# Fused attention and two expert layers on one core: one-hot work spread over more groups, the maxima's row written in two halves, gate steps moved forward

## The chip, the core and the metric

The kernel runs on one core of one Trainium2 chip. The metric is the device time of one launch in microseconds (us). The core has five engines with queues of their own: TensorE (PE, with its weight loads as PEld), VectorE (DVE), ScalarE (ACT), GpSimd (POOL) and SyncE (SP, which here only issues DMAs). Each engine takes its instructions in the order in which the program issues them, and waits on semaphores for the others.

## The reference

The kernel computes three layers in one launch: an attention whose queries are pooled in twos, a layer that sends each token to its best expert (2,304 tokens, 8 experts), and a soft mixture of experts over the result.

```python
q_pool = q.reshape(B, H, S // 2, 2, D).mean(axis=3)            # B=4, H=8, S=1152, D=64
scores = scale * np.matmul(q_pool, k.transpose(0, 1, 3, 2))
scores = scores - np.max(scores, axis=-1, keepdims=True)
attn = np.exp(scores); attn = attn / (attn.sum(-1, keepdims=True) + 1e-9)
x = (attn @ v) -> [B * S/2, H * D]                             # 2304 tokens of 512
logits = x @ w_gate + modality_bias[modality_id]; e = argmax(logits)
x = gate_w[:, None] * (relu(x @ w1[e]) @ w2[e])                # each token, its expert alone
return soft_moe(x)                                             # dispatch and combine by softmax
```

## The kernel before

**Tiling.** The attention goes over 16 pairs of heads, p = 0 to 15, four pairs to a batch (HP = 4), so pairs 0, 4, 8 and 12 are the first of their batches. A pair has 36 positions, pos = 0 to 35: two halves of the queries (u), nine blocks of 128 keys (c), two heads (j). At each position the program issues two matmuls for the scores (S1 at line 251 and S2 at line 257, both into one `sc` bank), the exponential on ScalarE (line 261), then whatever the table `work` holds for that position, then one step from `queue`, then one-hot steps, and, at positions 2, 8, 14, 20, 26 and 32, a group: twelve P·V matmuls (line 271) and three additions on GpSimd for the row sums (line 284). Everything is issued by hand in this order, and each engine keeps it.

**The maxima.** While pair p is worked on, the row maxima of the scores of later pairs are found in 27 pieces each: a matmul into a bank `mps` (lines 197 to 202) and a reduction by VectorE (line 204). At positions 29, 30, 31, 33, 34 and 35 of pairs 1 to 13 the pieces belong to pair p+2. At position 29 `maxred` puts the maxima of pair p+1 together, and at position 32 `maxrow` turns them with two transposes into a bank `nps` (line 220) and writes them with three multiplications by a mask into five rows of QL, which S2 of pair p+1 reads: one of 1024 columns for both heads (line 222), then one of 64 columns for each head (line 225). In pair 0 this happens at position 35, three positions later, as the `late` of line 566 says.

**The banks.** `mps`, `nps`, and the banks of `fin0` (`sg`), `fin1` (`sgT`), `fin2` (`tp`), `ranks` (`rp`) and `table` (`tbp`) are tiles with the one tag `mx`, of which there are three. They are handed out in turn: the fourth tile asked for takes the bank of the first and its first matmul waits until the first has been read for the last time. At position 33, behind the maxima's piece, `fin2(p, 0)` takes such a bank, in pairs that are not the first of their batch.

**Routing.** Behind the last pair of a batch, at position 18 (RT) of pairs 4, 8 and 12, `route` hands out the small steps that choose the experts of that batch's tokens, and `in_order` puts them into `queue`: `choose` (logits, their maximum, the winner), `gates` (an exponential on ScalarE, four small steps on VectorE, the last of which writes into `xr`, and a DMA that stores `xr` into `xs`), `place` (`ranks` with nine small matmuls, five small steps on VectorE, 24 one-hot steps on ScalarE at lines 372 and 373, and `table` with six matmuls), and `count` (two small steps on VectorE, lines 409 and 410). `rest` stands for empty steps. From `queue` one step is issued at positions with pos % 3 < 2 in pairs 4, 8, 12 and behind 12, and at even positions from 8 on in the others. One-hot steps are no callables of the queue; they are taken four at a time ahead of a group. The first two batches thus send their 24 one-hot steps into the groups at positions 26 and 32 of pair 5 (9) and 2, 8, 14 and 20 of pair 6 (10), and `table` and `count` come behind them at positions 22, 24 and 26 of pair 6 (10). `fin2(p - 1, 0)` at position 7 (FC) of pairs 5, 9 and 13 writes into the next batch's `xr`, of which there is one buffer.

Of the kernel before, what the change touches and what calls it, by code (L numbers as in the profile page):

```python
# [17 lines left out]
HP = H // 2  # L18
# [19 lines left out]
HPOS = 4  # L38
NI = N // 128
NB = E * (N // TS)  # L40
NHOT = 4
XW = DM + 8
QSTEP = 2
GS = 3
LAG = 3
# [11 lines left out]
MR = (29, 32)  # L57
# [4 lines left out]
RT = 18  # L62
# [23 lines left out]
def attention(ctx, tc, g):  # L86
# [8 lines left out]
    V = nc.vector  # L95
# [16 lines left out]
    mask = cp.tile([69, 5, 128], F32, name="mask")  # L112
    wgbd = cp.tile([128, HP, 2 * E], F32, name="wgbd")
    ahead = g["ahead"] = Ahead(tc, g, KS, KH, QS, QL, KX, QX, KC, KL, QLc, QC, VT)
    pairs = [(b, hp) for b in range(B) for hp in range(HP)]
    n = len(pairs)
# [18 lines left out]
    def load_v(p):  # L135
        b, hp = pairs[p]
        nc.sync.dma_start(out=st[p]["v"], in_=vT[b, hp])
# [77 lines left out]
    def maxrow(p):  # L215

        ql = st[p]["QL"]
        nps = ps.tile([128, 512], F32, name="nps", tag="mx", bufs=3)
        for j in range(2):
            nc.tensor.transpose(nps[:69, j * 128:(j + 1) * 128], MXZ[:, j, :], ident)  # L220
        nv = nps[64:69, 0:256].rearrange("p (j c) -> p j c", j=2)
        V.tensor_mul(ql[64:69, :, 0:512].rearrange("p j (a c) -> p j a c", a=4),  # L222
                     nv.unsqueeze(2).to_broadcast([5, 2, 4, 128]), mask[64:69, 0:4].unsqueeze(1).to_broadcast([5, 2, 4, 128]))
        for j in range(2):
            V.tensor_mul(ql[64:69, j, 512:576], nv[:, j, 64 * j:64 * j + 64], mask[64:69, 4, 0:64])

    def maxrow0(p, spans):

# [57 lines left out]
    def group(p, g_):  # L286
        steps = range(GS * g_, GS * g_ + GS)
        for step in steps:
            PV(p, step)
        for step in steps:  # L290
            if (p, step) != (n - 1, 2 * NKB - 1):
                accadd(p, step)
# [129 lines left out]
    def in_order(r, select=None):  # L422
        choose, place, count, gates = r

        rest = [lambda: None] * 3
        if select is None:
            return choose[:4] + rest[:2] + gates + choose[4:] + rest[:1] + place + count
        expert, rows = select
        place = place[:1] + count + rest + expert + [lambda i=i: ahead.fetch(i) for i in range(2)] + place[1:]
        return choose[:3] + rest + gates + choose[3:] + rest + place + rows[:1] + rest + rows[1:]  # L430

    def first():

# [100 lines left out]
    nc.sync.dma_start(out=wgbd[0:64, :, 0:E], in_=wg[0])  # L534
    nc.sync.dma_start(out=wgbd[64:128, :, E:2 * E], in_=wg[1])
    consts = g["route_consts"]()
    queue = []
    for p in range(n + 1):
        work = {}

        def at(pos, *fs):
            work[pos] = work.get(pos, []) + list(fs)

        mp = lambda q, m: (lambda: maxpiece(q, m))
        NP = len(pieces)
        if p == 0:
            for i, m in enumerate(range(NP0, NP)):
                at(P0[0] + i * P0[1] // 8, mp(0, m))
            at(P0[0] + P0[1] + 1, lambda: maxred(0, [3, 4]))
            at(P0[0] + P0[1] + 2, lambda: maxrow0(0, [(288, 384), (384, 512), (512, 576)]))  # L550
            for i, m in enumerate([24, 25, 26] + list(range(24))):
                at(P1[0] + i * P1[1] // NP, mp(1, m))
            for i in range(3):
                at(33 + i, mp(2, 24 + i))
        elif p + 1 < n:
            for pos, m in zip(MA1, range(24)) if p == 1 else zip(MA, range(3, 24)):
                at(pos, mp(p + 1, m))
            if p + 2 < n:
                for pos, m in zip(MB, (24, 25, 26, 0, 1, 2)):
                    at(pos, mp(p + 2, m))  # L560
        if p + 2 < n:
            for pos, f in zip(PREP0 if p == 0 else PREP, prep(p + 2, nc.gpsimd if p == 0 or p >= HP and p % HP < 2 else None)):
                at(pos, f)
        if p < n:
            if p + 1 < n:
                late = 3 if p == 0 else 0
                at(MR[0] + late, lambda: maxred(p + 1, [0, 1, 2, 3, 4]))
                at(MR[1] + late, lambda: maxrow(p + 1))
            late = 4 if p in (0, n - 1) else 2 if p >= HP and p % HP == 0 else 0
            at(FA[0] + late, lambda: fin0(p, 0))  # L570
            at(FA[1] + late, lambda: fin1(p, 0))
            if pairs[p][1]:
                at(FA[2], lambda: fin2(p, 0))
        if p > 0:
            if pairs[p - 1][1] == 0:
                at(FC, lambda: fin2(p - 1, 0))
            fb = FE if p < 4 else FB if p < n - HP else FZ
            at(fb[0], lambda: fin0(p - 1, 1))
            at(fb[1], lambda: fin1(p - 1, 1))
            if p < n:  # L580
                at(fb[2], lambda: fin2(p - 1, 1))
                if pairs[p - 1][1] == HP - 1:
                    at(RT, lambda: queue.extend(in_order(route(pairs[p - 1][0]), ahead.select() if p == n - HP else None)))
        if p == n - 2:
            for i in range(2, 6):
                at(AF2[i - 2], lambda i=i: ahead.fetch(i))
            for i in range(6):
                at(6 * i + 2, lambda i=i: ahead.split(i))
        if p == n - 1:
            at(0, lambda: ahead.fetch(6), lambda: ahead.fetch(7))  # L590
            at(14, lambda: ahead.load_x(0), lambda: ahead.load_x(1))
            at(26, lambda: ahead.turn(0))
            at(28, lambda: ahead.turn(1))
            at(29, ahead.gates)
            for i in range(6):
                at(6 * i + 2, lambda i=i: ahead.split(6 + i))
        if p == n:
            group(n - 1, 2 * NKB // GS - 1)
            assert not queue
            mm, ev = ahead.mm, ahead.ev  # L600

            def both(*fs):
                return [f[i] for i in range(max(map(len, fs))) for f in fs if i < len(f)]

            mm(0)
            ev(0)
            fin0(n - 1, 1)
            mm(1)
            fin1(n - 1, 1)
            ev(1)  # L610
            choose, place, count, gates = route(B - 1)
            ta, tb = g["make_tasks"](ps, count)
            rest = gates[1:]
            run = lambda fs: [f() for f in fs]
            run(choose[:3])
            mm(2)
            run(both(choose[3:], gates[:1]))
            fin2(n - 1, 1)
            ev(2)
            mm(3)  # L620
            place[0]()
            ta[0]()
            ev(3)
            mm(4)
            mm(5)
            table = place.pop()
            chain = both(place[1:], ta[1:], rest)
            for i, f in enumerate(chain):
                f()
                if i in TAIL:  # L630
                    u = 4 + TAIL.index(i)
                    ev(u)
                    if u < 6:
                        mm(u + 2)
            mm(8)
            mm(9)
            table()
            mm(10)
            tb[0]()
            cut = lambda u: (lambda: ahead.split(u))  # L640
            g["rest"] = [cut(12), cut(13), lambda: mm(11), cut(14), cut(15)] + [lambda u=u: mm(u) for u in range(12, 16)] + [lambda: ev(15)]
            break

        units = [(u, c, j) for u in range(2) for c in range(NKB) for j in range(2)]
        for z in units[:3]:
            S1(p, *z)
        for pos, z in enumerate(units):
            if pos >= 3:
                S1(p, *z)
            S2(p, *z)  # L650
            for f in work.get(pos, []):
                f()
            if p and pos % CST == 0 and consts:
                consts.pop(0)()
            if queue and pos >= (8 if p < n - 3 else 0) and (pos % 3 < 2 if p % HP == 0 or p > n - HP else pos % QSTEP == 0) and callable(queue[0]):
                queue.pop(0)()
            if pos % (2 * GS) == LAG - 1:
                for _ in range(NHOT):
                    if queue and not callable(queue[0]):
                        queue.pop(0)[1]()  # L660
            if pos == LAG - 1 and p > 0:
                group(p - 1, 2 * NKB // GS - 1)
            elif pos >= 2 * GS and pos % (2 * GS) == LAG - 1:
                group(p, pos // (2 * GS) - 1)
            if pos == 3 and p + 3 < n:
                if p == 0:
                    load_v(2)
                load(p + 3)
# [1085 lines left out]
```

## Time and profile before

| | us |
|---|---|
| median of 3 runs (lowest, highest) | 811.82 (810.58, 812.17) |
| profiled execution, its own time | 811.47 |
| span of its trace, first to last instruction | 809.8 |
| TensorE busy | 779.9 (96% of the span) |
| VectorE busy | 566.6 (70%) |
| GpSimd busy | 544.2 (67%) |
| ScalarE busy | 461.5 (57%) |
| mean granted TensorE clock | 0.995 |

The attention fills the span from its start to about 500 us, the expert layers the rest. "Busy" of TensorE counts overlapping matmuls once, and their ends are modelled, so two starts that follow each other say more than a duration. A wait shown in brackets behind a row is idle time of that engine before it, with the instruction that ended it.

### The profile page before, as it was taken

What the parts mean: (1) busy time and instruction counts of PE and PEld (TensorE: products, weight loads), DVE (VectorE), ACT (ScalarE), POOL (GpSimd) and SP (SyncE); (2) the same over time, 40 slices, a digit from 0 to 9 for tenths busy, and PEclk for the clock granted to TensorE, in tenths of its full rate; (3) what the DMA queues carried; (4) which work ended last, traced back from release to release, by engine and by line L of the source; (5) the groups of instructions that cost most, each with busy time, mean ns of one, the idle gap of its engine ahead of it and who ended that gap; (6) DMA issues with size and microseconds to landing.
All of it is one profiled execution on the core that took longest, in us unless ns stands there. A gap on an engine that the chain in (4) does not pass through costs nothing. (4 is left out here: it accounts for less than half of the span.)

```text
span 809.8 us, 15857 instructions
## 1 busy us (share of the span) xinstructions
PE 779.9 (96%) x5674; PEld 595.9 (74%) x5674; DVE 566.6 (70%) x1168; ACT 461.5 (57%) x1096; POOL 544.2 (67%) x501
## 2 busy tenths in 40 slices
PE   5899999999999999999999999999999999999897
PEld 5667777767677777677766667798898689888456
DVE  7587777778787878777878786766766566665262
ACT  5446665666865667766556974355554555554133
POOL 6878899999888988888988964534644564451200
PEclk9999999999999999999999999999999999999998
DMA  9876648668645667564554220577777887866997
GB/s 324 230 200 157 170 137 207 168 178 191 145 142 158 163 182 182 139 172 139 134 149 122 79 80 1 185 272 260 259 271 263 291 303 269 290 206 239 333 413 238
DMA packets 57781, 162.80 MB, mean 201 GB/s; under 512 B 14442, under 2 KB 21914, under 8 KB 53594
## 3 DMA queue, kind: packets, MB, share of 16 engines
q1 hardware_dynamic: 41604, 98.05, 43.0%
q0 software_dynamic: 13648, 47.32, 17.3%
q10 hardware_dynamic: 2448, 16.39, 5.6%
q8 instruction: 46, 0.75, 0.4%
q14 instruction: 35, 0.29, 0.1%
HBM read 110.45 MB, written 10.89 MB: 150 GB/s over the span
## 5 line engine op out<-in xcount | busy, mean ns | idle before, releaser
L284 POOL TENSOR_TENSOR acc<-acc,e 128x576 f32<-128x576 f32 x214 | 315.2, 1473 | 23.7 <-ACT e L261 10.3
L261 ACT ACTIVATE e<-sc 128x288 f32<-128x288 f32 x576 | 223.7, 410 | 138.9 <-PE sc L257 115.9
L204 DVE TENSOR_REDUCE mxp<-mps 128x1 f32<-128x384 f32 x432 | 220.6, 549 | 94.3 <-PE mps L202 86.4
L251 PE MATMUL sc<-QS,KS 128*128 128x288 f32 x576 | 185.7, 330 | 3.3 <-ACT e L261 3.1
L257 PE MATMUL sc<-QL,KH 69*128 69x288 f32 x576 | 169.7, 297 | 1.5 <-DVE QL L222 1.2
L271 PE MATMUL pv<-e,V 128*64 128x288 f32 x1152 | 162.0, 417 | 0.0
L251 PEld LDWEIGHTS sc<-QS,KS 128*128 128x128 f32 x576 | 108.9, 190 | 56.5 <-issue 27.1
L202 PE MATMUL mps<-KS,QS 128*128 128x384 f32 x384 | 134.8, 355 | 11.8 <-ACT QS L467 7.0
L743 POOL DMA_INDIRECT wraw<-in_w,widx x72 | 73.3, 1018 | 101.4 <-DVE wlo L765 73.9
L271 PEld LDWEIGHTS pv<-e,V 128*64 128x64 f32 x1152 | 74.4, 137 | 60.5 <-issue 22.5
L257 PEld LDWEIGHTS sc<-QL,KH 69*128 69x128 f32 x576 | 108.9, 189 | 2.0 <-DVE QL L222 1.4
L765 DVE TENSOR_TENSOR wlo<-wraw,whi 128x512 fp32r<-128x512 f32 x136 | 90.3, 687 | 26.1 <-ACT whi L764 23.5
L764 ACT CAST whi<-wraw 128x512 fp32r<-128x512 f32 x136 | 79.4, 619 | 15.4 <-DMA wraw<-in_w,widx 11.6
L202 PEld LDWEIGHTS mps<-KS,QS 128*128 128x128 f32 x384 | 74.1, 194 | 15.2 <-ACT QS L467 7.4
L773 PE MATMUL hp<-xh,whi 128*128 128x256 f32 x256 | 73.0, 285 | 0.0
L775 PE MATMUL hp<-xh,wlo 128*128 128x256 f32 x256 | 71.8, 280 | 0.2 <-DVE wlo L765 0.2
L774 PE MATMUL hp<-xl,whi 128*128 128x256 f32 x256 | 71.5, 279 | 0.0
L282 POOL TENSOR_TENSOR acc<-e 128x576 f32<-128x576 f32 x31 | 44.7, 1441 | 36.1 <-ACT e L261 36.0
L780 ACT ACTIVATE hh<-hp 128x256 fp32r<-128x256 f32 x64 | 24.5, 383 | 74.1 <-PE hp L775 72.6
L781 DVE SCALAR_TENSOR_TENSOR hl<-hp,hh 128x256 fp32r<-128x256 f32 x64 | 27.2, 424 | 42.2 <-ACT hh L780 42.2
L787 PE MATMUL yp<-whi,hh 128*128 128x512 f32 x128 | 52.7, 412 | 0.0
L773 PEld LDWEIGHTS hp<-xh,whi 128*128 128x128 f32 x256 | 48.0, 188 | 4.4 <-ACT whi L764 1.6
(402 smaller groups left out, 1234.3 us busy)
## 6 DMA issues: line engine op xcount, KB each, us to landing
mw<-in_m2w SPq DMA_DIRECT2D x17, 1024.0 KB, 12.4
mw<-in_m2w ACTq DMA_DIRECT2D x15, 1024.0 KB, 5.6
V<-in_vT SPq DMA_DIRECT2D x16, 576.0 KB, 3.9
KX<-in_kT SPq DMA_DIRECT2D x15, 576.0 KB, 4.9
QX<-in_qT SPq DMA_DIRECT2D x15, 576.0 KB, 6.1
KS<-KC SPq DMA_DIRECT2D x30, 288.0 KB, 5.0
KH<-KC SPq DMA_DIRECT2D x30, 288.0 KB, 5.6
QS<-QC SPq DMA_DIRECT2D x60, 144.0 KB, 4.6
```

The lines of the kernel that those rows point to most:

```text
L202: nc.tensor.matmul(mps[:, :384], s["QS"][:, j, blk * 128:(blk + 1) * 128], s["KS"][:, j, ks], start=True, stop=True)
L204: V.reduce_max(s["mxp"][:, slot, t:t + 1], mps[:, :384], axis=AX.X)
L251: nc.tensor.matmul(sc[:, :NU], s["KS"][:, j, c * 128:(c + 1) * 128], s["QS"][:, j, u * NU:(u + 1) * NU], start=True, stop=False)
L257: nc.tensor.matmul(sc[:, :NU], s["KH"][0:69, j, c * 128:(c + 1) * 128], s["QL"][0:69, j, u * NU:(u + 1) * NU], start=False, stop=True)
L261: nc.scalar.activation(s["e", u, c][:, j], sc[:, :NU], AF.Exp, scale=SM)
L271: nc.tensor.matmul(pv[j * 64:(j + 1) * 64, :NU], s["v"][:, j, c, :], e[:, j], start=(c == 0), stop=(c == NKB - 1))
L284: eng.tensor_add(s["acc", u], s["acc", u], s["e", u, c])
L743: return nc.gpsimd.indirect_dma_start(out=out, out_offset=None, in_=src, in_offset=bass.IndirectOffsetOnAxis(ap=idx, axis=0))
L764: nc.scalar.copy(hi, x)
L765: nc.vector.tensor_sub(lo, x, hi.bitcast(F32))
L773: nc.tensor.matmul(hp, wh[:, c], xh[:, k], start=(k == 0), stop=False)
L775: nc.tensor.matmul(hp, wl[:, c], xh[:, k], start=False, stop=(k == DM // 128 - 1))
```

## The change

`NHOT` becomes a table by position: two one-hot steps ahead of the groups at positions 2, 14, 20 and 26, none at 8, four at 32. Only pair 14, for the third batch, still takes four everywhere. The one-hot steps have a list of their own (`hots`), which is opened by a new step `ready` at the end of `place`; `table`, and for the third batch the steps behind it, wait in `after` until the last one-hot step is out. `count` no longer stands behind `table`. For the first two batches the queue is `choose[:4]`, one empty step (two before), `gates`, `choose[4:]`, one empty step, `place`, `ready`, `count`. In pair 4 a queue step is issued at every position from 18 to 28 and none behind, where it was two of three positions up to 34. `maxrow` does its three multiplications as two halves, one for each head (512 and 64 columns): the first at once, the second one position later for p > 0, where `work` has it behind that position's piece of the maxima, and at the same position for p = 0.

```diff
-NHOT = 4
+NHOT = {2: 2, 8: 0, 14: 2, 20: 2, 26: 2, 32: 4}
@@ maxrow @@
-        V.tensor_mul(ql[64:69, :, 0:512].rearrange("p j (a c) -> p j a c", a=4),
-                     nv.unsqueeze(2).to_broadcast([5, 2, 4, 128]), mask[64:69, 0:4].unsqueeze(1).to_broadcast([5, 2, 4, 128]))
-        for j in range(2):
+
+        def half(j):
+            V.tensor_mul(ql[64:69, j, 0:512].rearrange("p (a c) -> p a c", a=4), nv[:, j].unsqueeze(1).to_broadcast([5, 4, 128]), mask[64:69, 0:4])
             V.tensor_mul(ql[64:69, j, 512:576], nv[:, j, 64 * j:64 * j + 64], mask[64:69, 4, 0:64])
+
+        half(0)
+        return lambda: half(1)
@@ in_order @@
+        hots.extend(f[1] for f in place if not callable(f))
+        table = [place.pop()]
+        place = [f for f in place if callable(f)]
+        ready = lambda: hot.append(True)
         if select is None:
-            return choose[:4] + rest[:2] + gates + choose[4:] + rest[:1] + place + count
+            return choose[:4] + rest[:1] + gates + choose[4:] + rest[:1] + place + [ready] + count, table
         expert, rows = select
-        place = place[:1] + count + rest + expert + [lambda i=i: ahead.fetch(i) for i in range(2)] + place[1:]
-        return choose[:3] + rest + gates + choose[3:] + rest + place + rows[:1] + rest + rows[1:]
+        place = place[:1] + count + rest + expert + [lambda i=i: ahead.fetch(i) for i in range(2)] + place[1:] + [ready]
+        return choose[:3] + rest + gates + choose[3:] + rest + place, table + rows[:1] + rest + rows[1:]
@@ the loop over pairs @@
+    def begin(now, later):
+        queue.extend(now)
+        after.extend(later)
...
-                at(MR[1] + late, lambda: maxrow(p + 1))
+                rows = []
+                at(MR[1] + late, lambda rows=rows: rows.append(maxrow(p + 1)))
+                at(MR[1] + late + (p > 0), lambda rows=rows: rows[0]())
...
-            if queue and pos >= (8 if p < n - 3 else 0) and (pos % 3 < 2 if p % HP == 0 or p > n - HP else pos % QSTEP == 0) and callable(queue[0]):
+            if queue and pos >= (8 if p < n - 3 else 0) and (pos < MR[0] if p == HP else pos % 3 < 2 if p % HP == 0 or p > n - HP else pos % QSTEP == 0):
                 queue.pop(0)()
-            if pos % (2 * GS) == LAG - 1:
-                for _ in range(NHOT):
-                    if queue and not callable(queue[0]):
-                        queue.pop(0)[1]()
+            if pos % (2 * GS) == LAG - 1 and hot:
+                for f in hots[:4 if p == n - 2 else NHOT[pos]]:
+                    hots.pop(0)()
+                if not hots:
+                    hot.clear()
+                    queue.extend(after)
+                    after.clear()
```

## Rows read from the trace of the kernel before

**Rows 1.** The page, part 1: busy time, share and instructions of each engine.

```profile
PE 779.9 (96%) x5674; PEld 595.9 (74%) x5674; DVE 566.6 (70%) x1168; ACT 461.5 (57%) x1096; POOL 544.2 (67%) x501
```

**Rows 2.** Stretches: from:to length, busy (instructions) by engine, TensorE clock, DMA share, GB/s.

```profile
30.00:40.00 10.00, 7.42 (x36) 5.27 (x36) 4.05 (x9) 3.74 (x10) 6.42 (x5) 0.83 0.83 276
...
170.00:232.00 62.00, 60.25 (x415) 43.69 (x415) 48.97 (x102) 43.60 (x111) 55.83 (x48) 1.00 0.71 183
```

**Rows 3.** Timeline (start, length), TensorE: transposes of position 32, pairs 2, 3, 6, 10.

```profile
109.30 0.38 PE L220 MATMUL nps<-ident,MXZ 128*69 128x128 f32 x2
...
137.70 0.38 PE L220 MATMUL nps<-ident,MXZ 128*69 128x128 f32 x2
...
227.80 0.38 PE L220 MATMUL nps<-ident,MXZ 128*69 128x128 f32 x2
...
345.01 0.38 PE L220 MATMUL nps<-ident,MXZ 128*69 128x128 f32 x2
```

**Rows 4.** Timeline, TensorE: pairs 6 and 9, one-hot wait, `table`, `ranks`.

```profile
210.97 0.40 PE L251 MATMUL sc<-QS,KS 128*128 128x288 f32 x1 [0.70 <-ACT e L261]
...
220.65 0.87 PE L366 MATMUL tbp<-rR,rA 96*72 96x256 f32 x6
221.36 0.30 PE L251 MATMUL sc<-QS,KS 128*128 128x288 f32 x1
...
299.17 0.26 PE L356 MATMUL rp<-oh,trir 96*96 96x48 f32 x1
...
300.06 0.71 PE L271 MATMUL pv<-e,V 128*64 128x288 f32 x4
```

**Rows 5.** One-hot lines: count, ns min/median/max, first and last start, forms.

```profile
L372 ACT ACTIVATE far<-i,rdf x36: 342/428/497, 193.8 to 466.1; 96x72 f32<-96x72 f32 x18, 96x256 f32<-96x256 f32 x18
...
L373 ACT ACTIVATE rA<-far,tok,ntok x18: 446/447/448, 194.2 to 465.7; 96x72 fp32r<-96x72 f32 x18
L373 ACT ACTIVATE rR<-far,ones x18: 507/510/512, 195.1 to 466.6; 96x256 fp32r<-96x256 f32 x18
```

**Rows 6.** Timeline, pair 4's end and pair 5's start, TensorE and VectorE.

```profile
168.63 0.34 PE L202 MATMUL mps<-KS,QS 128*128 128x384 f32 x1
...
169.43 0.35 DVE L225 TENSOR_TENSOR QL<-nps,mask 5x64 fp32r<-5x64 f32 x2
...
169.93 0.41 PE L202 MATMUL mps<-KS,QS 128*128 128x384 f32 x1 [0.24 <-DVE QL L225]
...
171.67 0.44 PE L202 MATMUL mps<-KS,QS 128*128 128x384 f32 x1 [0.49 <-DVE mxp L204]
```

**Rows 7.** Timeline, VectorE, pair 9, position 8: `fin2` of the batch before.

```profile
296.06 0.55 DVE L332 TENSOR_TENSOR xr<-tp,rs 96x384 f32<-96x384 f32 x1 [1.50 <-DMA xs<-xr]
```

**Rows 8.** `count`'s two lines, as rows 5.

```profile
L410 DVE TENSOR_TENSOR run<-run,sm x3: 1075/1366/1369, 224.4 to 417.9; 96x8 fp32r<-96x8 f32 x3
...
L409 DVE TENSOR_REDUCE sm<-oh x3: 229/239/240, 222.5 to 417.2; 96x8 f32<-96x48 f32 x3
```

**Rows 9.** The maxima's row, two lines, as rows 5.

```profile
L222 DVE TENSOR_TENSOR QL<-nps,mask x15: 1222/1222/1222, 54.7 to 464.9; 5x1024 fp32r<-5x1024 f32 x15
...
L225 DVE TENSOR_TENSOR QL<-nps,mask x30: 211/211/213, 55.8 to 466.2; 5x64 fp32r<-5x64 f32 x30
```

**Rows 10.** Timeline, pair 3, positions 32 to 34, TensorE and VectorE.

```profile
138.43 1.22 DVE L222 TENSOR_TENSOR QL<-nps,mask 5x1024 fp32r<-5x1024 f32 x1
...
139.58 0.35 DVE L225 TENSOR_TENSOR QL<-nps,mask 5x64 fp32r<-5x64 f32 x2
...
139.99 0.34 PE L202 MATMUL mps<-KS,QS 128*128 128x384 f32 x1
...
140.36 0.56 DVE L204 TENSOR_REDUCE mxp<-mps 128x1 f32<-128x384 f32 x1 [0.44 <-PE mps L202]
...
140.76 0.34 PE L202 MATMUL mps<-KS,QS 128*128 128x384 f32 x1
...
140.95 0.55 DVE L332 TENSOR_TENSOR xr<-tp,rs 96x384 f32<-96x384 f32 x1
```

## What I predict, and why

> **What bounds the kernel now.** I began with the page: TensorE is busy 96% of the span, the next engines 70% and less [rows 1]. Then the attention by stretches: from 170 to 232 us TensorE is busy 60.25 of 62 at the full 2.4 GHz, the others leave room [rows 2]. So in the attention a microsecond in which TensorE stands still is lost for good, and work on another engine costs only what TensorE waits for it. The third view is a clock by pairs, the starts of the maxima's transposes at position 32, one per pair: an ordinary pair takes 137.70 - 109.30 = 28.40 [rows 3]. From pair 3 to pair 6 it is 90.10, against 3 x 28.40 = 85.20; from 6 to 10 it is 117.21, against 113.60 [rows 3]. The two batches' routing therefore costs 4.90 + 3.61 = 8.51. The last view, the timeline, says what ends the single waits.
>
> **One-hots.** Of the 8.51, the matmuls stay: `table` pushes the next S1 by 221.36 - 220.65 = 0.71, `ranks` the next group by 300.06 - 299.17 = 0.89 [rows 4], twice each, 3.20 together. 5.31 could go. A group of four one-hot steps occupies ScalarE for two `far` (one of each width, 0.43 on the mean) and one `rA` and one `rR`, 0.45 and 0.51: about 1.8 [rows 5]. ScalarE has little to do while TensorE is in a P·V group, but at position 8 it also makes two casts, and the S1 behind the group shows it: 0.70 idle ended by an exponential [rows 4]. Counted between starts of S2 rather than by the modelled ends, the four-step groups of a batch cost 0.98 at position 8, 0.48 at 2, some 0.6 and 0.2 at 26 of pairs 5 and 9, and nothing at 14, 20 and 32. That makes 3.7 for both batches. A group that takes 1.8 with 0.48 too many has room for 1.3; two steps need at most 1.0 (a `far` and an `rR`). So the new table should leave nothing at 2, 14, 20 and 26, and position 8 is free of them: 3.7 gone, bounds 2.9 (if position 26 still waits for the step ahead of it on VectorE) and 3.7. The steps that move into pair 7 (11) meet the same groups and cost nothing; `table` moves one pair on and costs its 0.71 there.
>
> **Gate steps.** The maximum's matmul at position 35 of pair 4 waits 0.24 for the maxima's row, and the one of pair 5's position 1 waits 0.49 for VectorE [rows 6], because small gate steps stand in VectorE's queue between the last pieces. With the steps issued at positions 18 to 28 they lie in front of the group at 26, in which VectorE has no piece to do. I count 0.9 (0.15 and 0.75 between starts), bounds 0.6 and 0.9. Nothing stands behind them on SP until the loads of pair 5, so the store of `xr` simply comes earlier, and its reader at position 8 (1.50 of VectorE's time in pair 9 [rows 7]) is released earlier; in pair 8 by one step alone. TensorE lost about 0.35 by it in pairs 5 and 9: 0.7 gone, bounds 0.35 and 0.7. The exponential of the gates waits on ScalarE for the subtraction three steps ahead of it, with the exponentials of the scores behind it; VectorE is some 0.5 behind there, so I count nothing, bounds 0 and 0.5. Together one-hots and gates give back 3.7 + 0.9 + 0.7 = 5.3, all of the 5.31.
>
> **Count.** Its addition of eight numbers takes 1.08 to 1.37, where its reduction takes 0.24 [rows 8]. Today it runs behind the group at 26. It moves to position 30 of pair 5, where it only pushes the row's first half into idle time, and to 28 of pair 9, ahead of the step that puts the maxima together: there the transposes of position 32, and the P·V group behind them, wait. I take 0.6, bounds 0 and 1.3, since how long it stands depends on what GpSimd is doing. The Trainium skill ("SBUF — State Buffer", section "Who interferes with whom") says why that may be: a VectorE instruction with two SBUF inputs is shut out while a GpSimd instruction that reads SBUF runs. By that rule alone the term would be as long as what is left of one row-sum addition.
>
> **The maxima's row.** This is the large term. Now all three multiplications follow each other at position 32: 1.22 us for 1024 columns and 0.21 for 64 [rows 9], and they run from 138.43 to 139.93, under the P·V group; the bank `nps` is free before TensorE starts position 33's piece at 139.99 [rows 10]. After the change the second half is queued on VectorE behind position 33's reduction, which can't start before that piece is there, at 140.36 [rows 10]. Until the second half is done, `nps` stays taken. Who wants it? The three banks go round: `nps`, then the piece of 33, then `fin2`'s `tp`, then the piece of 34, which needs the bank of `nps`. In pairs without `fin2` there (4, 8 and 12) it is the piece of 35. That this wait exists is seen today: at the end of pair 4, where the row was late, the piece of 35 waited for its last multiplication and started 0.15 behind it (169.43 + 0.35 = 169.78; 169.93) [rows 6].
>
> Its price, from pair 3: the next VectorE instruction can start 0.59 behind the reduction's start (140.95 - 140.36) [rows 10]. A multiplication of 512 columns is not in the trace; between 211 ns at 64 columns and 1222 at 1024 [rows 9] the line gives 0.68, and since the 64 started 139.58 - 138.43 = 1.15 behind a 1.22 [rows 10], the next follows at 0.61. Then 0.21, and 0.15 to the matmul: 140.36 + 0.59 + 0.61 + 0.21 + 0.15 = 141.92, where it starts at 140.76 today [rows 10]. That is 1.16, with S1, S2 and the rest of TensorE's queue behind it. Pairs 1 to 13 have these pieces. Ten of them (1 to 3, 5 to 7, 9 to 11, 13) pay 1.16. In the other three the wait sits one position later: in pair 4 the piece of 33 starts at 168.63 [rows 6], so its reduction at 169.00 (0.37 later, as in pair 3), and the piece of 35 could start at 169.00 + 1.56 = 170.56 instead of 169.93, 0.63 more; in pairs 8 and 12, which have no wait there, 0.45 x 2 behind the piece of 33 it would have started 1.04 sooner. Sum: 11.6 + 0.63 + 2.08 = 14.3. Below, if instructions on VectorE overlap more closely (0.47 instead of 0.59), 12.7; above, 15.5. Pair 14 has no pieces left there, and in pair 0 the halves follow each other at once: head 0 comes sooner, head 1 no sooner, nothing.
>
> The Trainium skill ("Perfetto Trace Analysis", section "Optimizing Scalar/DVE Operations") speaks for the change: where VectorE isn't full but makes gaps on other engines, breaking up instructions can let work finish sooner. In this trace the unbroken row makes a gap at the end of pair 4 alone [rows 6]; by that rule the time would be that of the first rival.
>
> **Sum.** 811.47 (the profiled execution; 0.35 below the median of the runs, which I leave aside) - 5.3 + 0.6 + 14.3 = 821.1; I say 821.0. With the terms' bounds it is 817 to 823.5.
>
> **Rivals.**
> 1. The bank isn't missed: the second half gets done without holding up a piece, because the reduction of 33 is no barrier in fact. Then only the gains are left, 811.47 - 5.3 + 0.6 = 806.8. For it: VectorE is idle until 140.36 [rows 10]. Against it: the queue's order, and the wait of pair 4 [rows 6]. 10%.
> 2. The bank is missed, but TensorE gets half of it back, since what it waits for later is then further along (VectorE's and GpSimd's backlog at the start of the next pair). 811.47 - 5.3 + 0.6 + 7.1 = 813.9; 7%. Against it: an ordinary pair has almost no wait to win back, 60.25 busy of 62 even in a stretch with routing [rows 2].
> 3. The repeated gaps bring TensorE's clock down. From 30 to 40 us, where it stood still longer, the granted clock was 0.83 [rows 2]; 13 times the 1.7 us that this stretch lost would be 22, so 843. Against it: 1.00 from 170 to 232 with the gaps of today in it [rows 2]. 2%.
>
> **How the numbers follow.** Forecast 81%, rivals 10, 7 and 2. Faster by over 0.2% (about what a measurement of this kernel can tell from no change) is below 810.2: the first rival, 0.10. Slower is above 813.4: the forecast, the third and most of the second, 0.87. Between them 0.03. The range reaches from 813.0, so that the second rival is in it, to 824.5, one over the forecast's own end.
>
> **What would show it.** The pieces at position 34 of ten pairs (35 in pairs 4, 8 and 12) with a wait of 0.6 to 1.2 ended by the 64-column multiplication; an ordinary pair of 29.5 instead of 28.4; no wait for exponentials at positions 5 and 11 of pairs 6 and 10, and none at the start of pair 5; the 512-column multiplication at 0.68. If pairs 1 to 3, which no routing touches, keep 28.4, the large term is wrong, and the first rival holds.

## The result, and the profile after

The changed kernel takes 818.03 us (median of 6 runs, 815.72 to 819.34) against 811.82 for the kernel before: ratio 1.0078, interval 1.0066 to 1.0090, so 6.3 us slower. One of the six runs of the kernel before took 1237.32 and is left out as slow; the other five lie between 810.58 and 813.65. The profiled execution takes 817.55, with a span of 815.8 (811.47 and 809.8 before). The forecast of 821.0 had the direction and its range held the time; the two large terms were not what I took them for, as the experiments show.

The page: TensorE stays the bound, and is busy 3.3 us more, though its instructions are the same in number.

```profile
PE 783.2 (96%) x5674; PEld 596.9 (73%) x5674; DVE 563.0 (69%) x1183; ACT 464.6 (57%) x1096; POOL 542.3 (66%) x501
```

The clock by pairs, which answers to [rows 3] (start, length; the transposes of position 32 in pairs 2, 3, 6 and 10):

```profile
109.53 0.38 PE L220 MATMUL nps<-ident,MXZ 128*69 128x128 f32 x2
...
138.41 0.38 PE L220 MATMUL nps<-ident,MXZ 128*69 128x128 f32 x2
...
227.31 0.38 PE L220 MATMUL nps<-ident,MXZ 128*69 128x128 f32 x2
...
346.03 0.38 PE L220 MATMUL nps<-ident,MXZ 128*69 128x128 f32 x2
```

An ordinary pair went from 28.40 to 28.88, though nothing but the row was changed in it. From pair 3 to pair 6 it is 88.90 (90.10 before), from 6 to 10 it is 118.72 (117.21). So routing gives back more than the row takes in the first batch, and not in the second.

TensorE's waits from 56 to 500 us (line and what ended it: us in total, times, longest), the changed kernel (its lines 254, 260, 264 and 335 are 251, 257, 261 and 332 of the kernel before):

```profile
PE mps L202 <- DVE QL L225: 2.4, 10, 0.2
PE mps L202 <- DVE mxp L204: 1.9, 3, 1.0
PE sc L254 <- ACT e L264: 1.7, 2, 1.5
PE mps L199 <- DVE mxp L204: 1.0, 2, 0.7
...
PE nps L220 <- DVE MXZ L213: 0.4, 1, 0.4
```

and the kernel before:

```profile
PE sc L251 <- ACT e L261: 3.1, 7, 0.8
PE mps L202 <- DVE mxp L204: 1.2, 2, 0.8
...
PE mps L202 <- DVE QL L225: 0.2, 1, 0.2
```

The seven waits for exponentials have become two. In their place stand ten waits for the 64-column multiplication (one in each pair that has `fin2` at position 33: 1 to 3, 5 to 7, 9 to 11 and 13) and more waits for reductions. VectorE has taken ScalarE's place as what TensorE waits for.

Pair 3 again, positions 32 to 35, as [rows 10], now with the second half:

```profile
139.14 0.69 DVE L224 TENSOR_TENSOR QL<-nps,mask 5x512 fp32r<-5x512 f32 x1
...
139.75 0.21 DVE L225 TENSOR_TENSOR QL<-nps,mask 5x64 fp32r<-5x64 f32 x1
...
140.70 0.34 PE L202 MATMUL mps<-KS,QS 128*128 128x384 f32 x1
...
141.07 0.56 DVE L204 TENSOR_REDUCE mxp<-mps 128x1 f32<-128x384 f32 x1 [1.11 <-PE mps L202]
...
141.66 0.69 DVE L224 TENSOR_TENSOR QL<-nps,mask 5x512 fp32r<-5x512 f32 x1
...
141.68 0.19 PEld L202 LDWEIGHTS mps<-KS,QS 128*128 128x128 f32 x1 [0.29 <-DVE mxp L204]
141.68 0.45 PE L202 MATMUL mps<-KS,QS 128*128 128x384 f32 x1
...
142.28 0.21 DVE L225 TENSOR_TENSOR QL<-nps,mask 5x64 fp32r<-5x64 f32 x1
...
142.52 0.55 DVE L335 TENSOR_TENSOR xr<-tp,rs 96x384 f32<-96x384 f32 x1
...
142.63 0.41 PE L202 MATMUL mps<-KS,QS 128*128 128x384 f32 x1 [0.24 <-DVE QL L225]
```

VectorE now stands idle for 1.11 in front of position 33's reduction, where it was 0.44, and the second half follows at 141.66, as foretold. But the piece of position 34 starts at 141.68, when the second half has only just begun: it does not wait for the bank of `nps`. Its weight load waited 0.29 for the reduction of position 33's piece, which ends at 141.07 + 0.56 = 141.63, so it has taken that piece's bank. The piece of 35 is the one that waits for `nps`. The banks are thus not handed out in the order in which tiles are asked for, as I wrote ahead of the prediction.

Between starts of S2 the changed pairs compare thus (pairs with several causes are taken apart by the positions at which the starts differ):

| where | us, after minus before |
|---|---|
| positions 34 and 35 of the ten pairs with `fin2` there, 0.47 each | +4.7 |
| pair 13, positions 0 to 5 (VectorE late behind pair 12's second half) | +1.3 |
| pair 14 (one-hots wait for the tokens' places; behind that a lower clock) | +2.0 |
| pair 4, position 31, and pair 8, position 31 (gate steps ahead of the maxima) | +1.5 |
| pair 9, position 32 (the count ahead of the maxima) | +0.6 |
| start of pair 5 (-0.4), start of pair 9 (+0.3), other small ones in pairs 5 and 9 (+0.4) | +0.3 |
| one-hots: pair 5 (-0.6), pair 6 (-1.4), pair 9 (-0.2), pair 10 (-1.5) | -3.7 |
| `table`, from pairs 6 and 10 to 7 and 11 | 0 |
| pair 0 and before, pair 1, and what follows pair 15 | -0.7 |
| sum, and the difference of the spans | +6.0 |

The waits for the third batch, in pairs 12 to 14. VectorE at the seam of pairs 12 and 13, first the last gate step in the kernel before, then the changed kernel:

```profile
405.74 0.18 DVE L417 COPY xr<-sm 96x48 f32<-96x48 f32 x1
```

```profile
408.16 0.69 DVE L224 TENSOR_TENSOR QL<-nps,mask 5x512 fp32r<-5x512 f32 x1
408.78 0.21 DVE L225 TENSOR_TENSOR QL<-nps,mask 5x64 fp32r<-5x64 f32 x1
409.02 0.98 DVE L420 COPY xr<-sm 96x48 f32<-96x48 f32 x1
```

The second half pushes the copy back, there it takes 0.98 instead of 0.18 beside an addition on GpSimd, and the piece of position 1 of pair 13 waits 0.95 for VectorE. The start of pair 14, first a step on the tokens' places in the kernel before, then VectorE and ScalarE in the changed kernel:

```profile
438.76 0.15 DVE L396 TENSOR_SCALAR rdi<-rdi 96x6 int32<-96x6 int32 x1
```

```profile
443.19 1.75 DVE L399 TENSOR_SCALAR rdi<-rdi 96x6 int32<-96x6 int32 x1
444.86 1.01 DVE L204 TENSOR_REDUCE mxp<-mps 128x1 f32<-128x384 f32 x2
445.79 0.64 DVE L400 CAST rdf<-rdi 96x12 f32<-96x12 int32 x1
```

```profile
446.47 0.36 ACT L375 ACTIVATE far<-i,rdf 96x72 f32<-96x72 f32 x1 [1.55 <-DVE rdf L400]
```

The step takes 1.75 instead of 0.15, the tokens' places (`rdf`) come later, the one-hot steps queued on ScalarE ahead of the exponentials wait 1.55 for them, and the S1 behind waits 1.50 for an exponential. A small delay on VectorE has become a long one on TensorE, by way of a third engine's queue. And it does not end there. TensorE behind that wait, and the stretch from 449.0 to 452.4 (its TensorE clock is the 0.50):

```profile
448.89 0.52 PE L254 MATMUL sc<-QS,KS 128*128 128x288 f32 x1 [1.50 <-ACT e L264]
```

```profile
449.00:452.40 3.40, 3.40 (x14) 2.63 (x16) 1.22 (x3) 2.31 (x7) 3.30 (x3) 0.50 0.39 152
```

The granted clock is 0.50 there, so 1.2 GHz, with TensorE busy throughout; from 430 to 449 it was 1.00. Positions 6 to 8 of pair 14 take 4.41 instead of 2.97, so 1.4 of pair 14's 2.0 stand in this stretch. In the kernel before, the wait at this place is 0.79 and the clock stays at 1.00. The four kernels that have the second half one position later all show the fall behind a wait of 1.50, and take 4.41 to 4.55 for these positions (4.87 where `fin2`'s transposes stand there too); the other eight have 1.00 and 2.95 to 2.97.

### The profile page after: what moved, and what is told of

It reads as the page before. It is cut to its first block, busy times and chain, and to the rows that moved or that the text cites. A ratio compares the mean times of both kernels' runs of the same rounds, so it can differ in the third digit from the quotient of the medians.

```text
span 815.8 us, 15870 instructions
## 1 busy us (share of the span) xinstructions
PE 783.2 (96%) x5674; PEld 596.9 (73%) x5674; DVE 563.0 (69%) x1183; ACT 464.6 (57%) x1096; POOL 542.3 (66%) x501
## 5 line engine op out<-in xcount | busy, mean ns | idle before, releaser
L254 PE MATMUL sc<-QS,KS 128*128 128x288 f32 x576 | 182.2, 327 | 1.8 <-ACT e L264 1.7
L202 PE MATMUL mps<-KS,QS 128*128 128x384 f32 x384 | 137.2, 361 | 15.5 <-ACT QS L474 7.1
```

The source lines that it names most:

```text
L202: nc.tensor.matmul(mps[:, :384], s["QS"][:, j, blk * 128:(blk + 1) * 128], s["KS"][:, j, ks], start=True, stop=True)
L254: nc.tensor.matmul(sc[:, :NU], s["KS"][:, j, c * 128:(c + 1) * 128], s["QS"][:, j, u * NU:(u + 1) * NU], start=True, stop=False)
```

## The experiments

Each was timed against the kernel before on its own chip; ratios are those, us are the ratio times 812.

**The row's split alone**, on the kernel before:

```diff
+        half(0)
+        return lambda: half(1)
...
+                at(MR[1] + late, lambda rows=rows: rows.append(maxrow(p + 1)))
+                at(MR[1] + late + (p > 0), lambda rows=rows: rows[0]())
```

> The kernel before with the row's split alone. Theory A (the second half keeps the maxima's bank and VectorE behind position 33's reduction, and TensorE waits at positions 34 and 35 of ten pairs, 0.48 us each in the trace of after): 812.0 + 4.8, and up to 3 more where VectorE is late for the third batch (pairs 13 and 14), so 816.8 to 820. Theory B (the split is free; what the change lost, it lost by the gate steps and the count, which now stand in front of the maxima on VectorE): 812, within 1.

Measured 1.0112 (1.0094 to 1.0130): 9.1 slower. Theory B falls. The ordinary pairs are 28.84 to 28.89 long, the starts of pairs 13 and 14 cost 3.3 by the starts of S2, pair 9's start 1.4, where a gate step on VectorE meets the second half, and pair 9 has a wait of 0.9 for a DMA into QB besides.

**All but the split**: the changed kernel with the row written as before.

```diff
-        half(0)
-        return lambda: half(1)
+        V.tensor_mul(ql[64:69, :, 0:512]...)   # and the two of 64 columns
...
+                at(MR[1] + late, lambda: maxrow(p + 1))
```

> The changed kernel with the row written as before, all else as changed. Theory A: the one-hots give back 3.8 and pair 5's start 0.5, gate steps cost 1.6 (pairs 4 and 8) and the count 0.6 (pair 9): 812.0 - 2.1 = 809.9, 808.5 to 811. Theory B: about 817 to 818, as the changed kernel.

Measured 0.9967 (0.9955 to 0.9980), 2.7 faster than before. Split and rest together, +9.1 and -2.7, make 6.4; the changed kernel measures 6.3. The split is the whole loss.

**The row's transposes in another bank**, the changed kernel with nothing else altered; the instructions of all engines and their order are the same.

```diff
-        nps = ps.tile([128, 512], F32, name="nps", tag="mx", bufs=3)
+        nps = ps.tile([128, 512], F32, name="nps", tag="pv", bufs=2)
```

> The changed kernel with the maxima's transposes in a bank of the P.V tiles, which has one free at position 32; the instructions and their order stay the same on every engine. If the bank is what is missed (theory A's first half): the waits at 34 and 35 vanish, 4.8 less than the changed kernel, about 813.3. If it is VectorE's order, that the pieces' reductions come later behind the second half: no change, about 818. Between them, a share for each.

Measured 1.0087 (1.0070 to 1.0105): nothing is won. TensorE at the end of pair 3 and the start of pair 4 with this bank:

```profile
141.27 0.34 PE L202 MATMUL mps<-KS,QS 128*128 128x384 f32 x1
...
141.71 0.34 PE L202 MATMUL mps<-KS,QS 128*128 128x384 f32 x1
...
142.61 0.30 PE L260 MATMUL sc<-QL,KH 69*128 69x288 f32 x1
...
142.93 0.19 PEld L202 LDWEIGHTS mps<-KS,QS 128*128 128x128 f32 x1 [0.26 <-DVE xr L335]
...
143.21 0.30 PE L260 MATMUL sc<-QL,KH 69*128 69x288 f32 x1
...
143.39 0.19 PEld L202 LDWEIGHTS mps<-KS,QS 128*128 128x128 f32 x1 [0.17 <-DVE mxp L204]
```

The pieces of 34 and 35 start 0.44 behind each other without a wait. But the first two pieces of pair 4 are late, since their weight loads wait for VectorE, one for `fin2`'s step and one for a reduction: from S2 to S2 it is 0.60 and 0.46 where it was 0.32 and 0.31. The first six positions take 4.47 instead of 4.03, so the 0.45 stand there now. My first theory, that the bank is what is missed, falls. A bank decides where TensorE stops; how long is decided by VectorE, which has 0.9 us of work more between position 33 and the next pair's position 2, with a reduction for every piece there.

**The halves together**, both at position 32, all else as in the changed kernel:

```diff
-                at(MR[1] + late + (p > 0), lambda rows=rows: rows[0]())
+                at(MR[1] + late, lambda rows=rows: rows[0]())
```

> The changed kernel with the second half right behind the first, at position 32 in every pair. If the loss comes from where the second half stands (0.9 us of VectorE's work moved from under the P.V group to behind position 33's reduction): the waits at positions 34 and 35 vanish and VectorE is in time for pairs 13 and 14, so as the kernel without the split: 0.997 of before, 808 to 809. If it comes from there being four multiplications instead of three (0.2 us more on VectorE per pair): 1.006 to 1.009 as the changed kernel.

Measured 0.9976 (0.9967 to 0.9985), as without the split (0.9967), within the intervals. The four multiplications take 1.57 on VectorE, the three of before 1.50 [rows 10], both under the P·V group:

```profile
136.49 0.69 DVE L224 TENSOR_TENSOR QL<-nps,mask 5x512 fp32r<-5x512 f32 x1
...
137.10 0.21 DVE L225 TENSOR_TENSOR QL<-nps,mask 5x64 fp32r<-5x64 f32 x1
...
137.24 0.68 DVE L224 TENSOR_TENSOR QL<-nps,mask 5x512 fp32r<-5x512 f32 x1
...
137.85 0.21 DVE L225 TENSOR_TENSOR QL<-nps,mask 5x64 fp32r<-5x64 f32 x1
...
138.43 0.56 DVE L204 TENSOR_REDUCE mxp<-mps 128x1 f32<-128x384 f32 x1 [0.37 <-PE mps L202]
```

They are done at 138.06, ahead of position 33's reduction at 138.43, and the pair is back at 28.36 to 28.40. The same work, one position earlier, costs nothing: it is the place, and no property of the split.

**The other bank, and `fin2` moved** from position 33 to position 7 of the next pair, up to pair 13:

```diff
-            if pairs[p][1]:
+            if pairs[p][1] and p > n - 3:
                 at(FA[2], lambda: fin2(p, 0))
...
-            if pairs[p - 1][1] == 0:
+            if p - 1 <= n - 3:
                 at(FC, lambda: fin2(p - 1, 0))
```

> The kernel with the maxima's row in a bank of the P.V tiles, and besides the step fin2 of position 33 (0.55 us of VectorE, three transposes) moved to position 7 of the next pair, where VectorE has room, in pairs up to 13. New theory (VectorE is behind from position 33 to the next pair's position 2, and TensorE waits wherever its next bank is not yet read): the 0.45 at the start of ten pairs vanish, 4.5 to 6 less, ratio to before 1.001 to 1.003. If VectorE's amount of work is not it: 1.008 as without the move.

Measured 1.0051 (1.0038 to 1.0064), 2.9 less than without the move, where I expected 4.5 to 6. By the starts of S2 the first six positions of an ordinary pair fell from 4.47 to 4.33 only. I had forgotten that `fin2` gives TensorE work too: with its transposes gone, positions 33 to 35 take 0.33 less, so VectorE lost 0.55 of work and 0.33 of the time to do it in. What is left agrees with a backlog on VectorE; that it explains the whole 2.9 is not shown, since the pairs' starts account for 1.4 of it.

**The one-hot table alone**, on the kernel before (`table` and `count` behind the last one-hot step):

```diff
-NHOT = 4
+NHOT = {2: 2, 8: 0, 14: 2, 20: 2, 26: 2, 32: 4}
```

> The kernel before with the new one-hot table alone (table and count behind the last one-hot step, one pair later; the row and the gate steps as before). If the four-step groups held up TensorE by ScalarE: 812.0 - 3.8 = 808.2, 807.5 to 809. If ScalarE's steps were hidden: 812.

Measured 0.9953 (0.9935 to 0.9971), 3.8 faster. TensorE's waits from 56 to 500 us keep two for exponentials, both in pair 14, whose batch still has four steps to a group:

```profile
PE mps L202 <- DVE mxp L204: 1.3, 2, 0.8
PE sc L251 <- ACT e L261: 1.0, 2, 0.8
```

**The gate steps alone**, on the kernel before:

```diff
-            return choose[:4] + rest[:2] + gates + ...
+            return choose[:4] + rest[:1] + gates + ...
...
+            if queue and ... (pos < MR[0] if p == HP else pos % 3 < 2 if ...)
```

> The kernel before with the gate steps' new places alone (pair 4 dense from 18 to 28, one empty step less; four one-hots per group, the row as before, table and count last). From the traces: 0.9 back at pair 5's start, 0.6 lost in pair 8, where a gate step meets a GpSimd addition ahead of the maxima: -0.3, so 0.998 to 1.001. If the gate steps carry the loss of the changed kernel: 1.004 and more.

Measured 1.0012 (1.0003 to 1.0021): nothing won, and 1.0 slower by the ratio. The 0.75 at pair 5's start are back, but the piece at position 25 of pair 5 now waits 0.5 for VectorE, and its one-hots come later, so that positions 24 to 29 of pair 5 take 6.41 where it was 5.41; pair 8 takes 0.63 more. Pair 4 loses nothing here.

**One-hots and the first batch's gate steps**, the second batch's gate steps, row and count as before:

> The parts that paid: the new one-hot table, the gate steps' new places behind the first batch alone (second batch as before), the row and the count as before. One-hots -3.8, pair 5's start -0.9: 810.9 - 4.7 = 806.2, ratio 0.994. If the gains don't add up: 0.9953 as with the one-hots alone.

Measured 0.9947 (0.9934 to 0.9960), not to be told from the one-hots alone. The trace says where the gain went: against the one-hots alone, 0.76 are won at pair 5's start and 0.77 lost at position 25 of the same pair, where the piece waits 0.50 for VectorE as in the run before. Besides, pair 9 has a wait of 1.0 for a DMA into QB at position 29, which the one-hots alone don't have.

**Two one-hots at position 2 for the third batch too**, the last two in pair 15, first on the one-hot table alone:

```diff
-                for f in hots[:4 if p == n - 2 else NHOT[pos]]:
+                for f in hots[:4 if p == n - 2 and pos > 2 else NHOT[pos]]:
```

> The one-hot table alone, and for the third batch too: two steps instead of four ahead of pair 14's group at position 2, the last two ahead of pair 15's at 2, so its table comes at pair 15's position 3. If the four steps behind a late position of the tokens hold ScalarE at pair 14's start (1.06 at position 5 in the traces): 0.8 to 1.0 less than the one-hot table alone, ratio 0.994. If what stands behind the table (the ahead rows for the expert layer) is then missed by the gathers of pair 15: 0.996 or more.

Measured 0.9955 (0.9941 to 0.9969): nothing won over the table alone. By the starts of S2 pair 14 went from 30.88 to 30.04, and pair 15 takes 0.72 more. But pair 15's is no wait: the six matmuls of `table` moved there, from position 33 of pair 14, which is 0.71 shorter for it. What was won, 0.94 at position 5 of pair 14, was lost in pair 14 itself, to a new wait at position 32:

```profile
459.06 0.41 PE L220 MATMUL nps<-ident,MXZ 128*69 128x128 f32 x2 [0.80 <-DVE MXZ L213]
```

**The same with the first batch's gate steps:**

> The same for the third batch, on the kernel with the one-hot table and the first batch's gate steps: 0.9947 - 0.0012 = 0.9935 if the gains add up; 0.9947 if not.

Measured 0.9950 (0.9937 to 0.9964). This trace has no wait for QB in pair 9, but the 0.77 at position 25 of pair 5 and the 0.80 at position 32 of pair 14. The gains don't add up beyond the one-hot table's: 4 us faster than the kernel before is what I found, and the one-hot table alone has it.

## Why the prediction was right or wrong

**What bounds the kernel**: right. The loss and the gains are TensorE's waits, and 1.4 of a lower clock behind one of them; the terms of the table above make up the difference of the spans.

**One-hots**: right in place and size. 3.7 were said; 3.8 came alone, and the moved steps cost nothing at positions 2, 14, 20 and 26. Position 26's wait went too, the better of the bounds. Pair 5's 0.6 of it is not the one-hots' alone: it is gone with the split alone as well, which has four steps ahead of that group.

**Gate steps**: wrong. I counted 0.9 and 0.7 given back, and the experiment shows none. The 0.7 were a misreading. VectorE's wait for the store of `xr` [rows 7] was real, and is gone in the changed kernel (pair 5 here; pair 9 has none either):

```profile
178.56 0.56 DVE L335 TENSOR_TENSOR xr<-tp,rs 96x384 f32<-96x384 f32 x1
```

but the 0.34 between two starts of S2 at position 7 of pairs 5 and 9 stayed. They are `fin2`'s own three transposes, which other pairs have at position 33. I had taken work for a wait because both stood at the same place. The 0.9 came in part and were lost again, by a price that I left out: a gate step that stands ahead of the maxima at position 29 instead of behind them. VectorE in pair 4 of the changed kernel:

```profile
163.96 1.40 DVE L418 TENSOR_SCALAR sm<-sm 96x6 f32<-96x6 f32 x1
165.40 0.19 DVE L419 RECIPROCAL sm<-sm 96x6 f32<-96x6 f32 x1
165.50 0.52 DVE L204 TENSOR_REDUCE mxp<-mps 128x1 f32<-128x384 f32 x1
165.94 1.39 DVE L420 COPY xr<-sm 96x48 f32<-96x48 f32 x1
```

GpSimd beside it:

```profile
163.91 1.42 POOL L287 TENSOR_TENSOR acc<-acc,e 128x576 f32<-128x576 f32 x1
...
165.87 2.90 POOL L287 TENSOR_TENSOR acc<-acc,e 128x576 f32<-128x576 f32 x2
```

An addition of six numbers and a copy of 48 take 1.40 and 1.39, and end with the GpSimd additions that began just before them (163.91 + 1.42 = 165.33; 165.87 and half of 2.90, 167.32), while the reduction and the reciprocal between them take 0.52 and 0.19. The piece of position 31 then waits 0.68 for VectorE. The Trainium skill ("SBUF — State Buffer", section "Who interferes with whom") names copies and `tensor_scalar` among the operations that can be shut out so, and reductions not; these rows agree. I had used this for the count alone. Which position pays depends on which step meets an addition. With the gate steps alone, the same copy, at the same place in the program, is

```profile
162.95 0.32 DVE L417 COPY xr<-sm 96x48 f32<-96x48 f32 x1
```

and pair 4 loses nothing; pair 5 pays instead, 0.77 at position 25. Pair 4's loss, 0.95 by the starts of S2, thus needs the gate steps and the second half together: the split alone doesn't have it either.

**Count**: right. 0.6 were said for pair 9; the transposes come 0.63 later between starts of S2, 0.41 by the bracket.

**The row**: right in mechanism up to VectorE's queue (the second half behind position 33's reduction; 0.69 for 512 columns against my 0.68), wrong in the step that follows, and so in price and in place. "The three banks go round": they don't. The piece of 34 got the bank of position 33's piece, whose last reader is issued ahead of the second half. The one trace row that I rested on, the wait of pair 4 [rows 6], fits both orders. So 1.16 for ten pairs became 0.47, and what I foresaw at position 35 of pairs 4, 8 and 12 did not come (there the next pair's start is late by 0.3 in pairs 5 and 9). And the bank does not set the price, as the run with the other bank shows; what fits all four runs (the split alone, the other bank, the halves together, `fin2` moved) is VectorE's backlog: 0.9 of new work where VectorE, in pair 3 of the kernel before, stood idle for 0.18 between position 33's reduction and the last one before the next group. That this gives just 0.47 is not worked out.

**Not foreseen**: 3.3 at the third batch, where pair 13 and pair 14 depend on small steps at the end of VectorE's queue. I had followed the second half to TensorE's next piece, and not to those who wait for VectorE one pair later, nor to the lower clock behind the longest of these waits. So 14.3 for the row were in truth 4.7 + 0.3 + 3.3 = 8.3 in this trace (9.1 alone), the gains 3.7 instead of 5.3 with 1.5 lost at the gates, and the sum came out 3 too high.

**The sum.** Its bounds were added up wrongly. By the terms' own bounds the least is 811.47 - 5.3 + 0 + 12.7 = 818.9 and the most 811.47 - 3.85 + 0.5 + 1.3 + 15.5 = 824.9, not 817 and 823.5, and the 818.0 measured lies below that. It is in the stated range, whose lower end I had put at 813.0 for the second rival. And that the forecast is only 3 off is in good part luck: the row cost 4.7 where I had put 14.3, and what closed most of the gap, pairs 13 and 14 and the loss at the gates, I had not foreseen.

**The rivals**: the first (no loss) is refuted by the split alone. The second, half of the loss won back, gave 813.9; the price was lower from the start, nothing was won back. The third, a lower clock in the attention, came once and not thirteen times: not behind the row's own waits, but behind pair 14's 1.50, where it cost 1.4, not 22. The page's mean of 0.995, the same as before, does not show it.

## What to carry to other kernels

Work on an engine that isn't the bound is free only as long as it lies in that engine's idle stretch. Here 0.9 us of VectorE's work moved by one position out of the shadow of a P·V group, and cost 9 us over 13 pairs, half of it where it stands and most of the rest further on, where small steps came late; the same split with both halves in the shadow cost nothing. Give another buffer only after it is shown that the buffer sets the length of the wait: here another bank moved the wait by two positions and won nothing. And before a gap between two starts is called a wait, look whether the program issues something there.

## What the runs showed of the hardware that I had not expected

TensorE's clock near 32 us differs from execution to execution. In pair 0 a piece waits for a DMA; how long it waits differs. In the kernel before, and with the one-hot table alone:

```profile
32.55 0.41 PE L202 MATMUL mps<-KS,QS 128*128 128x384 f32 x1 [2.91 <-DMA KS<-KL]
```

```profile
32.08 0.41 PE L202 MATMUL mps<-KS,QS 128*128 128x384 f32 x1 [2.49 <-DMA KS<-KL]
```

From 30 to 40 us the first has a mean granted clock of 0.83 [rows 2], with TensorE at 1.2 GHz for a part of it, the second of 1.00 (2.4 GHz throughout):

```profile
30.00:40.00 10.00, 7.89 (x50) 5.61 (x51) 5.82 (x12) 4.42 (x12) 6.83 (x5) 1.00 0.87 289
```

In twelve profiles of twelve kernels, six waited 2.9 to 3.7 there and have 0.83, six waited 2.3 to 2.6 and have 1.00. These lengths are no border: in pair 14 of the changed kernel the granted clock fell to 0.50 behind a wait of 1.50. In the two executions shown, positions 12 to 17 of pair 0 take 9.38 and 7.41. That is 1.97 more, of which the longer wait is 0.42. No edit touches this stretch, so I take it for chance, and for a part of the spread of a kernel's runs, whose mean clocks differ too (0.993 to 0.999 over 17 runs of the kernel before on one chip); why the wait differs is not shown. That is why differences of a microsecond were read from the pairs and from the ratios, not from two spans.
